# Attention and a squared-ReLU MLP on one core: earlier weight scans, row-tiled transposes in the second half, GpSimd sums tied to the softmax, float16 down products in four blocks

## Chip, cores and metric

The kernel runs on one core of one Trainium2 chip. The metric is the device time of one execution in microseconds (us). The kernel before takes 697.07 us (median of 3 runs, 697.04 to 697.47).

## What is computed

Attention over 4 batches, 8 heads, 576 positions and head size 64, with a bias from a small network on the positions, and then an MLP over the 2304 tokens. All inputs and outputs are float32.

```python
scores = scale * np.matmul(q, k.transpose(0, 1, 3, 2))
...
h = np.maximum(x @ w1 + b1, 0.0)
bias = h @ w2
scores = scores + bias.transpose(2, 0, 1)[None, :, :, :]
scores = scores - np.max(scores, axis=-1, keepdims=True)
attn = np.exp(scores)
attn = attn / (np.sum(attn, axis=-1, keepdims=True) + 1e-09)
return np.matmul(attn, v).astype(np.float32)
...
h = x @ w_in          # x: 2304 x 512, w_in: 512 x 2048
r = np.maximum(h, 0.0)
g = r * r
return (g @ w_out).astype(np.float32)   # w_out: 2048 x 512
```

## The kernel before, in words

**Units.** Attention is cut into units of one batch, one pair of heads and 128 query rows; a fifth unit of each pair holds the last 64 rows and is half as large. A *step* of the program handles one unit. The first half (steps 0 to 39) does batches 0 and 1 and also builds the bias; the second half (the loop from L1112, steps 40 to 82) does batches 2 and 3.

**First half.** A step multiplies q and k on TensorE (L425, into the PSUM tile `sp`, four banks). VectorE adds the bias and takes the row's extreme in one custom instruction per head (`reduce`, L438, tile `t` and column `negm`), ScalarE takes exp (L445, `p`). `transposes_by_rows` (L536) then transposes `p` in blocks of 64 rows and 128 columns (`half_block`, L534): two such blocks, in the upper and lower 64 rows of TensorE's array, go to two different PSUM banks. One last full block per unit, `pa` (L547), holds the columns of the tail. ScalarE copies the result to `pt` (L869), and `values` (L565) multiplies `pt` with v. Beside this run the pieces of the bias: masks (VectorE, L373), their products (TensorE, L383), and sums (ScalarE L388, VectorE L391, GpSimd L399). The order on TensorE is written by hand; at L856 `step` says what is issued in a step.

**Second half.** A step begins with the unit's scores. An even step then transposes the two units before it (`transposes`, L501): full blocks of 128 x 128 (L529), four to a bank. They use three banks (tags a, b, c), with `pa` of both units in the fourth (d), and the fourth group of blocks takes bank a again. ScalarE copies bank by bank (L1141). An odd step multiplies the transposed pair with v. The softmax of the step is issued after this. The tile `t` between VectorE and ScalarE has two buffers (`TB`). What is left of the engines is filled by a planner (`job` and `fill`, L946 to L964): each job is a list of pieces with an engine and a cost, and a step has so much `room` for VectorE and ScalarE. The jobs prepare the MLP. `scan` (L1009) takes the largest element of each w_in tile (VectorE, L204; 12 tiles here, 4 in steps 35 to 39 by `scan_first`), which sets a scale; `in_job` (L1084) splits w_in tiles into float16 high and low parts, with sums on GpSimd (`sums_in`, L738 to L740); `x_scaled` (L1035) does the same for the attention's result (`sums_x`, L797, on GpSimd; `high_x` L803, `low_x` L810).

**MLP.** 40 items, each a group of tokens and a block P (0 to 7) of the hidden columns. An item's up products (`products`, L1210, into `ha` and `hb`) are float16 products of high and low parts, in seven combinations (`sums`, L1214, adds them up again). `squares` and `parts_g` (L1240) make g = relu(h)^2 and split it into `gh` (ScalarE, L1246) and `gl` (VectorE, L1247), rounded float32 (`fp32r`). `down` (L1287, products L1302) adds gh·wh, gh·wl and gl·wh into `y`; 864 products of 128 x 512 in all. `leave` (L1260) takes `y` out. Tables (`lead_at`, `split_at`, `largest_at`, `raw_outs`, L1179 to L1187) say in which item a weight block is loaded and split. `high_out` and `rest_out` split w_out.

Of the kernel before, what the change touches and what calls it, by code (L numbers as in the profile page):

```python
# [27 lines left out]
AB = 2  # L28
# [43 lines left out]
MAGIC = 8388608.0  # L72

# [4 lines left out]
def attention_then_relu2_mlp(ctx: ExitStack, tc: tile.TileContext, q, k, v, cols, w_in, w_out, psi, xmat, dist, out):  # L78
# [11 lines left out]
    bank_p["p"] = aux_stack.enter_context(tc.tile_pool(name="aux", bufs=4, space=PSUM))  # L90

# [68 lines left out]
    def load_v(b, hp):  # L160
        t = att.tile([128, 5, 2, D], F32, name="v", tag="v", bufs=AB * HP)
        SP.dma_start(out=t, in_=v[b, hp])
        v_t[b, hp] = t
# [17 lines left out]
    small = keep.tile([128, 72], F32, name="small")  # L181
    used = [0]

    def column(w=1):
        used[0] += w
        return small[:, used[0] - w:used[0]]
# [32 lines left out]
    def power_of(ps_col):  # L219
# [3 lines left out]
        DVE.tensor_scalar(out=ti, in0=ti, scalar1=0x7F800000, scalar2=None, op0=ALU.bitwise_and)  # L223
        DVE.tensor_scalar(out=si, in0=ti, scalar1=-1.0, scalar2=266 * 2.0 ** 23, op0=ALU.mult, op1=ALU.add)
        DVE.tensor_scalar(out=isig, in0=top, scalar1=2.0 ** -12, scalar2=None, op0=ALU.mult)
# [7 lines left out]
    def top_w():  # L233
        m = column()
        mi = m.bitcast(I32)
        largest(wcols, m)
        DVE.tensor_scalar(out=m, in0=m, scalar1=HI_MIN, scalar2=HI_MAX, op0=ALU.max, op1=ALU.min)
        t = column()
# [194 lines left out]
    def reduce(u, n, negm, sp):  # L433
# [3 lines left out]
        t = att.tile([128, S], F32, name="t", tag="t", bufs=TB)  # L437
# [63 lines left out]
    def transposes(us, tags=None):  # L501
        next_tag = iter(tags) if tags else None
        groups = []
        pa = None
        for m, u in enumerate(us):
            p_of = p_t.pop(u)
            pt = att.tile([128, 9, 128], F32, name="pt", tag="pt", bufs=2)
            pt_t[u] = pt
            for h in range(2 if units[u][2] < TAIL else 1):
                groups.append((p_of, pt, h))  # L510
            groups.append((p_of, pt, None, m))
        if len(us) > 1:
            heads = [g for g in groups if g[2] is not None]
            groups = heads[:3] + [g for g in groups if g[2] is None] + heads[3:]
        last = []
        for p, pt, h, *m in groups:
            if h is None:
                if pa is None:
                    pa = bank("pa", "d" if tags and len(us) > 1 else next(next_tag) if tags else None)
# [207 lines left out]
    def high_out(n):  # L727
        copy_out(n)
        rest_out(n)
# [695 lines left out]
```

## Time and profile before

| | |
|---|---|
| median of 3 runs | 697.07 us |
| the profiled execution | 697.57 us |
| its span | 695.8 us |
| TensorE matmul (PE) | 676.8 us busy, 97% of the span |
| TensorE weight load (PEld) | 561.5 us, 81% |
| VectorE (DVE) | 549.9 us, 79% |
| ScalarE (ACT) | 473.2 us, 68% |
| GpSimd (POOL) | 196.5 us, 28% |

The span lies 1.8 us below the profiled execution's time, which counts what lies around the span. Busy time is the time in which an engine had at least one instruction at work; it is an average over three stages that do different work, so each stage is read by itself below. PE and PEld run side by side. Line numbers (L529) are those of the kernel before, unless the changed kernel is named. In a row, `out<-in` gives the tiles by the program's names, `x` the number of instructions; a number in brackets at the end of a timeline row is the idle time of the engine before it and what ended it.

### The profile page before, as it was taken

The numbers are of one execution on the slowest core, as the hardware profiler recorded it, in microseconds if no ns is written. First come the engines' busy times: TensorE is split into PE (matmuls) and PEld (weight loads), VectorE is DVE, ScalarE is ACT, GpSimd is POOL, SyncE is SP. The second block draws the span as 40 slices with busy tenths as digits, with TensorE's granted clock in tenths as the row PEclk, the third lists the DMA queues.
The fourth block names the chain that finished last, engine by engine and source line by source line (L and its number), as shares of the span: only waits on it lengthen the run. The fifth ranks groups of instructions, "written<-read, shape, count | busy, mean of one in ns | idle before, by whom it ended". The sixth has DMA issues, their size and how long they took to land.

```text
span 695.8 us, 17950 instructions
## 1 busy us (share of the span) xinstructions
PE 676.8 (97%) x7238; PEld 561.5 (81%) x7238; DVE 549.9 (79%) x1165; ACT 473.2 (68%) x960; POOL 196.5 (28%) x313
## 2 busy tenths in 40 slices
PE   6899999999999999999999999999999999999997
PEld 5578888887877878778788888888888888888886
DVE  8999989877788898998888969777477775567664
ACT  5678888888777989997666756766466664447221
POOL 6465545442112343653223205112020112001000
PEclk9999999999999999999999999999999999999999
DMA  6740000017476134111901443050057222633101
GB/s 188 205 128 13 20 2 3 2 63 206 152 266 196 55 116 131 47 33 57 367 2 62 152 167 122 14 214 1 1 194 291 106 77 106 227 121 122 62 1 31
DMA packets 31682, 75.16 MB, mean 108 GB/s; under 512 B 5616, under 2 KB 13936, under 8 KB 30576
## 3 DMA queue, kind: packets, MB, share of 16 engines
q1 hardware_dynamic: 31440, 73.76, 31.1%
q8 instruction: 57, 0.93, 0.6%
q14 instruction: 25, 0.20, 0.1%
q10 hardware_dynamic: 160, 0.26, 0.1%
HBM read 55.66 MB, written 18.35 MB: 106 GB/s over the span
## 4 chain that ended last, share of the span: by engine, by line
PE 86%; DVE 8%; ACT 2%; issue 2%; POOL 1%; DMA 0%; ACTq 0%; POOLq 0%; DVEq 0%
PE y L1302 29%; PE ha L1210 13%; PE sp L425 11%; PE px L565 10%; PE hb L1210 10%; PE bb L383 5%; PE pp L529 3%; PE pp L534 3%; DVE t L438 2%; DVE mask L373 1%; PE pa L547 1%; ACT pt L1141 1%; DVE bt L391 1%; ACT p L445 1%; DVE xT L496 0%
## 5 line engine op out<-in xcount | busy, mean ns | idle before, releaser
L1210 PEld LDWEIGHTS <-area 128*128 128x128 f16 x1680 | 147.7, 98 | 25.3 <-issue 8.4
L1302 PE MATMUL y<-w,gh 128*128 128x512 f32 x576 | 149.0, 398 | 0.6 <-ACT gh L1246 0.6
L1302 PEld LDWEIGHTS y<-w,gh 128*128 128x128 f32 x576 | 105.1, 188 | 22.2 <-ACT gh L1246 1.3
L438 DVE CUSTOM_DVE_ANT_0 t<-sp,area 128x576 f32<-128x576 f32 x144 | 104.2, 753 | 21.2 <-PE sp L425 10.3
L445 ACT ACTIVATE p<-t,negm 128x576 f32<-128x576 f32 x144 | 112.9, 794 | 2.7 <-DVE negm L438 2.1
L425 PE MATMUL sp<-k,q 64*128 64x288 f32 (+1 forms) x640 | 99.4, 428 | 5.5 <-DVE negm L438 3.9
L565 PE MATMUL px<-pt,v 128*64 128x128 f32 (+1 forms) x1600 | 92.2, 266 | 0.0
L565 PEld LDWEIGHTS px<-pt,v 128*64 128x64 f32 x1600 | 79.2, 137 | 10.7 <-ACT pt L1141 6.0
L1210 PE MATMUL ha<-area 128*128 128x256 f16 (+1 forms) x816 | 85.1, 260 | 0.7 <-DVE c L1227 0.7
L399 POOL TENSOR_TENSOR area<-bt,bt 128x256 f32<-128x256 f32 x72 | 65.9, 922 | 64.1 <-DVE bt L391 63.9
L1302 PE MATMUL y<-w,gl 128*128 128x512 f32 x288 | 79.0, 390 | 0.0
L425 PEld LDWEIGHTS sp<-k,q 64*128 64x128 f32 (+1 forms) x640 | 53.3, 176 | 25.5 <-issue 6.0
L1210 PE MATMUL hb<-area 128*128 128x256 f16 (+1 forms) x612 | 64.7, 260 | 0.0
L1302 PEld LDWEIGHTS y<-w,gl 128*128 128x128 f32 x288 | 54.1, 188 | 12.2 <-DVE gl L1247 0.2
L373 DVE TENSOR_TENSOR mask<-sdist,theta 128x1024 f16<-128x1024 f16 x81 | 57.3, 711 | 1.0 <-PE bb L383 0.8
L869 ACT COPY pt<-pp 128x512 f32<-128x512 f32 (+1 forms) x76 | 37.4, 544 | 24.9 <-PE pp L534 24.7
L383 PEld LDWEIGHTS <-mask 128*128 128x128 f16 x1296 | 45.9, 99 | 9.5 <-DVE mask L373 6.4
L383 PE MATMUL bb<-wmov,mask 128*128 128x64 f16 x1296 | 47.5, 193 | 5.5 <-DVE mask L373 4.7
L1141 ACT COPY pt<-pp 128x512 f32<-128x512 f32 x76 | 41.4, 601 | 12.8 <-PE pp L529 12.3
L1247 DVE TENSOR_TENSOR gl<-area,gh 128x512 fp32r<-128x512 f32 (+1 forms) x40 | 25.3, 668 | 27.3 <-ACT gh L1246 25.5
L738 POOL TENSOR_TENSOR raw<-wa 128x256 f32<-128x256 f32 x16 | 12.2, 761 | 120.9 <-issue 66.1
L388 ACT ACTIVATE bt<-bb,small 128x256 f32<-128x256 f32 x81 | 39.1, 486 | 7.1 <-PE bb L383 5.2
(164 smaller groups left out, 1062.2 us busy)
## 6 DMA issues: line engine op xcount, KB each, us to landing
raw<-in_w_in SPq DMA_DIRECT2D x32, 512.0 KB, 4.4
r<-in_w_out SPq DMA_DIRECT2D x16, 512.0 KB, 5.4
xs<-area SPq DMA_DIRECT2D x4, 1792.0 KB, 11.1
py<-o SPq DMA_DIRECT2D x12, 512.0 KB, 4.1
o<-py SPq DMA_DIRECT2D x12, 512.0 KB, 4.1
v<-in_v SPq DMA_DIRECT2D x16, 320.0 KB, 4.0
q<-in_q SPq DMA_DIRECT2D x32, 128.0 KB, 3.0
out<-o SPq DMA_DIRECT2D x8, 512.0 KB, 2.9
```

Of the source, the lines that this page charges most:

```text
L373: DVE.tensor_tensor(out=out, in0=win, in1=th, op=ALU.is_ge)
L383: PE.matmul(bb[:, 64 * (7 - r):64 * (8 - r)], lhsT=m[:, r], rhs=wmov[:, n], start=(n == 0), stop=(n == 1))
L388: ACT.activation(out=sv, in_=bv[:, 1], func=AF.Identity, scale=bscale)
L399: POOL.tensor_tensor(out=dst, in0=tw, in1=sw, op=ALU.add)
L425: mm = PE.matmul(out_t[to, x, :HALF], lhsT=qt[rows, cols], rhs=kt[rows, k0:k0 + HALF], start=True, stop=True)
L438: DVE.tensor_tensor_reduce(out=t.rearrange("p (x n) -> p x n", x=2), in0=sp[:, :, :HALF], in1=bias.rearrange("p (x n) -> p x n", x=2), sca ...
L445: ACT.activation(out=p[:, S * n:S * n + S], in_=t, func=AF.Exp, bias=negm[:, n:n + 1], scale=-1.0, accum_out=sums[:, 2 * ic + n:2 * ic + n ...
L565: PE.matmul(px[64 * h:64 * h + 64, 128 * m:128 * m + w], lhsT=vt[:, c, h], rhs=src, start=(c == 0), stop=(c == 4))
L869: ACT.copy(dst, src)
L1141: ACT.copy(*c)
L1210: PE.matmul(h[:, s, :w], lhsT=a, rhs=x, start=(k == 0), stop=(k == 5))
L1302: PE.matmul(y_t[n][k], lhsT=(gl if m == 2 else gh)[:, slot, o:o + 128], rhs=wl if m == 1 else wh, start=((n, P) in firsts and f == 0 and m ...
```

## The change

Five parts.

1. **Scans.** The 12 scans of w_in that were jobs of the second half are issued in steps 8 to 23 of the first half (`scan_corners`); the tiles are loaded from step 5 into four corners of the buffer `area`. The four of `scan_first` stay at its place. The second half's weight jobs begin at its first step (`begin`).
2. **Transposes.** `pair_by_rows` takes the place of `transposes` in the second half: half blocks as in the first half, banks a and b for the first unit, c and d for the second; then `pa` of both, into bank a, once ScalarE's copy of that bank is done.
3. **Buffers of `t`.** Four instead of two in the second half.
4. **GpSimd's sums.** `sums_in` and `sums_x` are issued just ahead of a step's softmax (a new slot "TT" of the planner, 2.0 us of room), and 26 one-column VectorE memsets make GpSimd wait until VectorE is there. The planner also keeps a count of how far GpSimd is behind.
5. **Float16 down products.** In blocks P = 4 to 7 the parts of g and w_out are float16, scaled by powers of two: gh·hi, gh·lo and gl·fine, where `fine` is hi/1024. This concerns 432 of 864 products. The scales need the largest element of eight w_out tiles (eight more scans on VectorE, in items 3 to 9), some 40 one-column VectorE instructions, five small products, eight more GpSimd and eight more ScalarE instructions on w_out tiles (the scaling and `fine`); the output is scaled as it leaves `y`.

```diff
+    scan_stack, scan_steps = ExitStack(), (8, 9, 11, 12, 14, 15, 17, 18, 20, 21, 22, 23)
...
+    def scan_corners(s):
+        if s == 5:
+            for k in range(4):
+                fetch(ins[k], corner[k])
+        if s in scan_steps:
+            k = scan_steps.index(s)
+            scan_w(k)
+            if k + 4 < CORNERS:
+                fetch(ins[k + 4], corner[k % 4])
...
+    def pair_by_rows(us, tags):
...
+            pp = [bank("pp", tag) for tag in tags[2 * m:2 * m + 2]]
+            n = 8 if units[u][2] < TAIL else 4
+            for c in range(n):
+                for x in range(2):
+                    half_block(pp[x][:, 64 * c:64 * c + 64], p, x, c // 4 * (S + 64) + c % 4 * 128)
+            for x in range(2):
+                yield pts[m][:, :n, 64 * x:64 * x + 64], pp[x][:, :64 * n].rearrange("p (c m) -> p c m", c=n)
+        pa = bank("pa", tags[0])
+        for m, u in enumerate(us):
+            PE.transpose(pa[:, 128 * m:128 * m + 128], p_t.pop(u)[:, S - 64:S + 64], ident)
+        for m, pt in enumerate(pts):
+            yield pt[:, 8], pa[:, 128 * m:128 * m + 128]
...
-                for m, c in enumerate(transposes(us, iter("bacb" if s == NA else "abca")) if us else ()):
+                for c in pair_by_rows(us, "bacd" if s == NA else "abcd") if us else ():
                     ACT.copy(*c)
...
+            t = soft_p["p"].tile([128, S], F32, name="t", tag="t", bufs=4)
...
-            ("POOL", 2.0, lambda: sums_in(n)),
+            ("TT", 1.45, lambda: sums_in(n, (0, 1), True)),
+            ("TT", 0.45, lambda: sums_in(n, (2,), True)),
...
+            fill(s, 4)
             for fn in sms:
                 fn()
...
+        t = home[n].tile([128, 3, 512], F16, name=f"w{n}", tag=f"w{n}", bufs=1)
+        hi, lo, fine = w_t[n] = [t[:, k] for k in range(3)]
+        POOL.tensor_scalar(out=a, in0=a, scalar1=oscale[0], scalar2=None, op0=ALU.mult)
+        ACT.copy(hi, a)
+        POOL.tensor_tensor(out=lo, in0=a, in1=hi, op=ALU.subtract)
+        ACT.activation(out=fine, in_=hi, func=AF.Identity, scale=1.0 / FINE)
...
+            if P >= NP // 2:
+                gl, gh = (mlp.tile([128, 4, 256], F16, name=x, tag=x, bufs=2)[:, 0:2, :w] for x in ("gl", "gh"))
+                g = c[:, 1 - f:4:2]
+                ACT.activation(out=gh, in_=g, func=AF.Identity, scale=1.0 / FINE)
+                DVE.scalar_tensor_tensor(out=gl, in0=gh, scalar=-FINE, in1=g, op0=ALU.mult, op1=ALU.add)
...
-                y_t[n][k], lhsT=(gl if m == 2 else gh)[:, slot, o:o + 128], rhs=wl if m == 1 else wh,
+                y_t[n][k], lhsT=(gl if m == 2 else gh)[:, slot, o:o + 128], rhs=(wh, wl, *fine)[m] if fine else (wh, wl, wh)[m],
```

**TensorE's order in an even step of the second half.** `sp` is the score tile, `pp` and `pa` the transposed blocks, `rp` a small product of the row sums. Before:

```order
L425 MATMUL sp<-k_4811,q_4814 128x288 x4
L474 LDWEIGHTS parts
L474 MATMUL rp<-ident_b,parts 128x128
L529 MATMUL pp<-ident,p 128x128 x12
L521 MATMUL pa<-ident,p 128x128 x2
L529 MATMUL pp<-ident,p 128x128 x4
L425 MATMUL sp<-k_4811,q_4814 128x288 x4
```

Now, with the line numbers of the changed kernel:

```order
L433 MATMUL sp<-k_4907,q_4910 128x288 x4
L485 LDWEIGHTS parts
L485 MATMUL rp<-ident_b,parts 128x128
L514 MATMUL pp<-ident,p 128x64 x32
L547 MATMUL pa<-ident,p 128x128 x2
L433 MATMUL sp<-k_4907,q_4910 128x288 x4
L566 MATMUL px<-pt,v 64x128 x20
```

Sixteen full blocks have become 32 half blocks, and the two `pa` blocks stand last, straight ahead of the next scores.

**VectorE's order in a step of the first half.** L438 (now L449) is the softmax pass; `mask` and `bt` belong to the bias; `xT` is the attention's result. Before:

```order
L438 ISA t,negm<-sp,area 128x576
L438 ISA negm 128x1
L438 ISA t,negm<-sp,area 128x576
L438 ISA negm 128x1
L373 TENSOR_TENSOR mask<-sdist,theta 128x1024
L391 TENSOR_TENSOR bt_2480<-bb,xc 128x256
```

Now:

```order
L449 ISA t,negm<-sp,area 128x576
L449 ISA negm 128x1
L449 ISA t,negm<-sp,area 128x576
L449 ISA negm 128x1
L209 TENSOR_REDUCE small<-area 128x1
L381 TENSOR_TENSOR mask<-sdist,theta 128x1024
L399 TENSOR_TENSOR bt_2501<-bb,xc 128x256
```

The scan (L209) has come in between the softmax and the bias work of the step.

**VectorE's order in a step of the second half**, in the changed kernel, at one of the memsets. `wa` is a w_in tile in preparation, `raw` the tile that GpSimd's sums go to:

```order
L205 SCALAR_TENSOR_TENSOR wa<-r_4403,wa 128x512
L206 SCALAR_TENSOR_TENSOR wa<-r_4403,wa 128x512
L750 MEMSET raw 128x1 x2
L449 ISA t,negm<-sp,area 128x576
L449 ISA negm 128x1
```

The memsets stand ahead of the softmax, and GpSimd's sums, which before began once their inputs were there, now begin after these.

## Rows read from the trace of the kernel before

**Rows 1.** Windows by stage: length, busy us (instructions) per engine, clock, DMA share, GB/s.

```profile
core 0: us, PE busy (x) PEld busy (x) DVE busy (x) ACT busy (x) POOL busy (x), PEclk, DMA share, GB/s
55.40:119.74 64.34, 64.33 (x1230) 55.51 (x1228) 58.16 (x142) 55.05 (x145) 31.94 (x34) 1.00 0.03 7
181.85:324.30 142.45, 139.24 (x1635) 112.40 (x1632) 125.48 (x319) 124.68 (x308) 51.17 (x110) 1.00 0.36 116
350.00:640.00 290.00, 290.00 (x1906) 243.07 (x1905) 211.36 (x340) 173.98 (x236) 48.66 (x56) 1.00 0.32 116
```

**Rows 2.** Timeline of PE, second half: start us, us, instruction.

```profile
258.63 1.24 PE L425 MATMUL sp<-k,q 64*128 64x288 f32 x8
259.87 1.48 PE L529 MATMUL pp<-ident,p 128*128 128x128 f32 x12
261.19 0.38 PE L521 MATMUL pa<-ident,p 128*128 128x128 f32 x2
261.41 0.60 PE L529 MATMUL pp<-ident,p 128*128 128x128 f32 x4
261.94 1.24 PE L425 MATMUL sp<-k,q 64*128 64x288 f32 x8
265.69 1.19 PE L425 MATMUL sp<-k,q 64*64 64x288 f32 x8
268.93 1.24 PE L425 MATMUL sp<-k,q 64*128 64x288 f32 x8
272.43 1.24 PE L425 MATMUL sp<-k,q 64*128 64x288 f32 x8
275.42 0.96 PE L425 MATMUL sp<-k,q 64*128 64x288 f32 x5
```

**Rows 3.** Timeline of VectorE and ScalarE, the same even step.

```profile
260.71 0.75 DVE L438 CUSTOM_DVE_ANT_0 t<-sp,area 128x576 f32<-128x576 f32 x1
260.57 0.59 ACT L1141 COPY pt<-pp 128x512 f32<-128x512 f32 x1 [0.23 <-PE pp L529]
```

**Rows 4.** Timeline of PE, first half.

```profile
111.90 0.66 PE L534 MATMUL pp<-ident,p 64*128 64x64 f32 x16
112.49 0.33 PE L547 MATMUL pa<-ident,p 128*128 128x128 f32 x1
```

**Rows 5.** Waits, second half: us in total, times, longest us.

```profile
ACT pt L1141 <- PE pp L529: 12.3, 15, 2.5
DVE t L438 <- ACT p L445: 7.2, 8, 1.6
```

**Rows 6.** Lines of PE and PEld, whole span: busy us, mean ns of one | idle before.

```profile
L529 PEld LDWEIGHTS pp<-ident,p 128*128 128x128 f32 x304 | 33.3, 140 | 4.5 <-issue 1.8 <-ACT p L445 1.6 <-ACT wa L195 0.4
L534 PEld LDWEIGHTS pp<-ident,p 64*128 64x128 f32 x544 | 22.5, 140 | 7.4 <-issue 1.3 <-ACT xT L576 0.9 <-ACT bt L388 0.4
L1302 PE MATMUL y<-w,gh 128*128 128x512 f32 x576 | 149.0, 398 | 0.6 <-ACT gh L1246 0.6
L1302 PE MATMUL y<-w,gl 128*128 128x512 f32 x288 | 79.0, 390 | 0.0
```

**Rows 7.** Timeline of PE, MLP.

```profile
520.13 1.98 PE L1302 MATMUL y<-w,gh 128*128 128x512 f32 x8
521.95 1.07 PE L1302 MATMUL y<-w,gl 128*128 128x512 f32 x4
522.86 2.79 PE L1210 MATMUL ha<-xT,area 128*128 128x256 f16 x24
525.49 2.13 PE L1210 MATMUL hb<-xT,area 128*128 128x256 f16 x18
527.37 1.40 PE L1302 MATMUL y<-w,gh 128*128 128x512 f32 x5
```

**Rows 8.** Lines of VectorE, second half.

```profile
L204 DVE TENSOR_REDUCE small<-raw 128x1 f32<-128x512 f32 x12 | 7.6, 680 | 0.0
L223 DVE TENSOR_SCALAR small<-small 128x1 int32<-128x1 int32 x3 | 0.5, 153 | 0.1
```

**Rows 9.** Timeline of VectorE, first half.

```profile
103.20 0.76 DVE L438 CUSTOM_DVE_ANT_0 t<-sp,area 128x576 f32<-128x576 f32 x1 [0.33 <-PE sp L425]
112.11 0.76 DVE L438 CUSTOM_DVE_ANT_0 t<-sp,area 128x576 f32<-128x576 f32 x1 [0.34 <-PE sp L425]
```

More of the change, by code (lines that the diff above doesn't have):

```diff
@@ L185, in column @@
         used[0] += w
-        return small[:, used[0] - w:used[0]]
+        return columns[0][:, used[0] - w:used[0]]
+    columns = [small]
     def lead_w(n, a, upto=7):
@@ L499, in scale_x @@
         times_rows(b, hp, *spread_rows(rows_t))
[L501 to L519, printed above, removed]
-                at = slice(128 * m[0], 128 * m[0] + 128)
-                PE.transpose(pa[:, at], p[:, S - 64:S + 64], ident)
-                last.append((pt[:, 8], pa[:, at]))
-                if len(last) == len(us):
-                    yield from last
-            else:
-                pp = bank("pp", next(next_tag) if tags else None)
-                for c in range(4):
-                    k0 = h * (S + 64) + 128 * c
-                    PE.transpose(pp[:, 128 * c:128 * c + 128], p[:, k0:k0 + 128], ident)
-                yield pt[:, 4 * h:4 * h + 4], pp.rearrange("p (c m) -> p c m", c=4)
     def half_block(dst, p, x, k0):
@@ L962, in fill @@
                     j[0] = s + lag(eng, j[1][0][0])
+                if eng == "POOL":
+                    behind[0] = max(behind[0], 3.2 * s) + cost
+                    if j[1] and j[1][0][0] != "POOL":
+                        j[0] = max(j[0], int(behind[0] / 3.2) + 1)
         for js in (jobs, norms):
@@ L1037, in x_scaled @@
         if n == 0:
[L1038 to L1039 removed]
+            free = [xT[b][:, HP - 1, 0:512] for b in range(AB, B)]
             for k, ms in enumerate(((3, 1, 7), (4, 6), (2, 5))):
@@ L1112, in attention_then_relu2_mlp @@
     with tc.manual_schedule():
-        job(NA + 1, *(("DVE", 0.68, lambda k=k: scan(k)) for k in range(SCANS, NF)))
+        job(NA, ("DVE", 0.75, begin))
         x_job(NA + 4, 0)
@@ L1195, in attention_then_relu2_mlp, with scan_out, squares_of @@
     c_t, g_t, y_t = {}, {}, {}
-    scales = []
+    columns[0], used[0] = xT[0][:, 0, 384:512], 0
+    ocols, beta, lead_root = column(len(late_outs)), column(NB), column(NB)
+    root, root_beta = column(NB), column(NB)
+    oscale, reach = [], []
+    xcols.extend(column(HP) for _ in range(AB, NB))
+    def scan_out(n):
+        k = late_outs.index(n)
+        largest(wraw_t[n][:, :, :, 1].bitcast(F32), ocols[:, k:k + 1])
+    def squares_of(dst, cols):
+        DVE.tensor_tensor(out=dst, in0=cols, in1=cols, op=ALU.mult)
@@ new lines, in scale_columns, with early_columns @@
+    def scale_columns(n):
+        if n < B - 1:
+            return overall(xcols[n])
+        cols = column(1 + HP)
+        squares_of(cols[:, 1:], xcols[n])
+        largest(xcols[n], cols[:, 0:1])
+        return cols
+    def early_columns():
+        cols = column(NF + (B - 1) * HP)
+        values_of(wcols, cols[:, 0:NF])
+        squares_of(cols[:, 0:NF], wcols)
+        for n in range(B - 1):
+            squares_of(cols[:, NF + HP * n:NF + HP * n + HP], xcols[n])
+        return cols
@@ new lines, in told_x, with then, told_out @@
+    def told_x(n):
+        def then(ps):
+            scale_of(n, ps[:, 0:1])
+            if n >= B - 1:
+                roots_of(n, n + 1, ps[:, 1:])
+            if n == B:
+                last_scales(B, NB)
+        return then
+    def told_out(ps):
+        oscale.extend(power_of(ps, 0x7F000000, 11))
+        r = column()
+        DVE.tensor_scalar(out=r.bitcast(I32), in0=oscale[0].bitcast(I32), scalar1=0.5, scalar2=58.5 * 2.0 ** 23, op0=ALU.mult, op1=ALU.add)
+        oscale.append(r)
+        last_scales(0, B)
```

189 lines of the change are left out of this document (122 added, 67 removed).

## Prediction

> **What bounds the kernel now.** I read the windows by stage first, because a saving is worth only what its own stage lets through [rows 1]. In the first half, from 55.40 to 119.74 us, PE is busy for 64.33 of 64.34 us, but VectorE for 58.16 as well: TensorE is the bound with 6.2 us of VectorE to spare. In the second half, from 181.85 to 324.30 us, PE is busy 139.24 of 142.45 us, VectorE 125.48 and ScalarE 124.68: again TensorE, by a thinner margin (3.2 us of it are idle). In the MLP, from 350 to 640 us, PE is busy 290.00 of 290.00 us and VectorE only 211.36. So time is to be had from TensorE in all three stages, and work that is put on VectorE is free in the MLP, nearly free in the first half and costly in the second. The clock is granted in full (1.00) in all three, so no term below is a matter of clock. Next I read the timelines, for the cost of one instruction where TensorE runs without a gap, start to start; the busy times in the groups of instructions overlap and are no price.
>
> **The change part by part.**
>
> *Down products in float16.* Before: from 520.13 to 522.86 us twelve products of 512 columns, 0.2275 us each [rows 7]. What a float16 product costs is read from the up products behind them: (525.49−522.86)/24 = 0.1096 us, and (527.37−522.86)/42 = 0.1074 us, for 256 columns. Twice that is 0.2148 to 0.2192 us, so 8.3 to 12.7 ns less for each. For 432 of the 864 products (576 and 288 in [rows 6]) this is 3.6 to 5.5 us, all of it on the bound engine. I take **−4.5**. The work that comes with it lies on VectorE (eight scans at 0.68 us [rows 8] = 5.4 us, and some 40 one-column instructions at 0.153 us = 6.1 us) and on GpSimd and ScalarE (eight each). It is hidden by the 290 − 211 = 79 us in which VectorE idles in the MLP, so it costs nothing. Were that cover gone, it would be up to 11.5 us.
>
> *Row-tiled transposes.* Before: twelve full blocks in 261.19−259.87 = 1.32 us, 0.110 us each [rows 2]. The first half shows the other form: eight pairs of half blocks in 112.49−111.90 = 0.59 us, 0.074 us for what a full block does [rows 4]. The 304 full blocks [rows 6] thus give at most 304 × 0.036 = 10.9 us; with all of TensorE's idle time in this stage, 3.2 us, on top it is 14.1, the upper end.
> How much arrives depends on what ends an even step next. An even step now lasts 261.94−258.63 = 3.31 us [rows 2]. Its scores start at 258.63; the second softmax pass on them ends at 260.71+0.75 = 261.46 [rows 3]. The next scores overwrite the banks which that pass reads, so the loop from scores to softmax to scores can't be shorter than 2.83 us and a start-up. The step with less to transpose (272.43 to 275.42) lasts 2.99 us, and I take that as the floor: a gain of 0.32 us where TensorE alone would give 16 × 0.036 = 0.58. Of the 20 even steps, 13 have full units on all sides: 4.2 us. The seven others (one of them 268.93−265.69 = 3.24 us, whose own softmax is half as long) I put at 0.2 us each: 1.3 us. The wait of VectorE for a buffer of `t` (7.2 us in 8 waits [rows 5]) goes with four buffers, but most of it only moves to the next wait for ScalarE; I take a fifth, 1.5 us.
> What is late next is ScalarE. Before, `pa` had a bank of its own; now it stands behind the copy of bank a, and behind it on TensorE stand the next scores. The first copy of a pair now starts at 260.57 and takes 0.59 us [rows 3], so bank a is free at 261.16. The row-tiled blocks start at 259.87 and 16 pairs end at 259.87 + 16 × 0.074 = 261.05. That is 0.1 us of waiting if ScalarE is on time, with 0.38 us of `pa` behind it: 261.54, still near the 261.62 that the floor allows. ScalarE is not always on time: I take off 1.0 us (0.05 us in each even step). Together 4.2 + 1.3 + 1.5 − 1.0: **−6.0**, between −2 (only half of the first term) and −14.1.
>
> *Scans into the first half.* Twelve scans at 0.68 us [rows 8] are 8.2 us of VectorE. In the second half this leaves an engine that isn't the bound there and gives nothing by itself. In the first half it meets 6.2 us of slack in the stretch of steps 9 to 23 [rows 1]. Part of the slack is waiting for the scores of the very step, 0.33 and 0.34 us before the first softmax pass [rows 9], and a scan behind the second pass can eat into that only if the mask behind it isn't needed at once. The scans are spread over 16 steps, so each step gets 0.5 us against 6.2/15 = 0.4 us of slack. I take **+1.5**, between 0 and 8.2 (no cover at all). The loads of the scans (512 KB each) are moved ahead on SP's queue; the DMA share there is 0.03 [rows 1], so they land in time and delay nothing.
>
> *Memsets ahead of the softmax.* 26 one-column instructions; the nearest row is the one-column one at 0.153 us [rows 8], so 0 to 4.0 us of VectorE. They stand where VectorE mostly waits for the scores. **0**. GpSimd is busy 51 of 142 us [rows 1] and has room to start later.
>
> The sum is 1.5 − 6.0 − 4.5 = −9.0 us, against the profiled execution 697.57 − 9.0 = 688.6. That execution lies 0.5 us over the median of the runs, 697.07, so against the median it is **688.1 us**.
>
> **The rivals.**
>
> *VectorE becomes the bound of the first half.* For: 58.16 + 8.2 is 66.4 us in a stretch of 64.34 [rows 1]. Against: single waits show VectorE catching up. Then the scans cost 8.2 instead of 1.5: 697.07 + 8.2 − 6.0 − 4.5 = 694.8 us. Chance 0.13; in a third of it the second half also gives little, and the time is no different from before.
>
> *The transposes give all they have.* If the next scores don't wait for the softmax, and TensorE's idle time closes too: 697.07 + 1.5 − 14.1 − 4.5 = 680.0 us. For: VectorE loses 8.2 us of work in this stage. Against: the 2.99 us of the lighter step. Chance 0.10.
>
> *Float16 gains nothing.* If TensorE takes a product of 512 columns at the same 0.2275 us in either type: 692.6 us. For: the difference per product is a few ns, and the up products differ in shape from the down ones. Chance 0.07.
>
> *The memsets are not covered.* 4.0 us come back: 692.1 us. Chance 0.03.
>
> *ScalarE is late, and TensorE stands (slower).* `pa` waits for ScalarE's first copy, and the scores of the next step are queued behind it, so each us by which the copy is late is lost on TensorE and then on VectorE. With a mean lateness of L in 20 even steps the cost is 20 × L: it passes the 9.0 us of gain at L = 0.45 us. At 0.6 us the time is 697.07 − 9.0 + 12.0 = 700.1 us. For: ScalarE is busy 125 of 142 us [rows 1]. Against: before, ScalarE waited for TensorE ahead of the copies in 15 of the pairs, 12.3 us in all [rows 5], so it has been early, 0.8 us on the mean. Chance 0.05.
>
> *Weight loads set the pace (slower).* The rows: 304 full blocks kept the weight load busy 33.3 us, 0.110 us each, and the 544 half blocks 22.5 us, 0.041 us each [rows 6]. If a half block needed a whole load of 0.110 us after all, 608 of them would take 66.9 us, 33.6 more: 697.07 + 1.5 + 33.6 − 4.5 = 727.7 us. Against: the 0.041 us, and the 0.59 us of the eight pairs [rows 4], into which 16 such loads (1.76 us) don't fit. Chance 0.02. The Trainium skill has the rule behind this rival (TensorE: Matmul & The Clock Gate, on LDWEIGHTS): "A 32×128 weight load takes the same time as a 128×128 weight load". By that rule alone halving the rows saves no load and doubles their number; the trace doesn't agree, at 0.041 against 0.110 us, so I keep the rows.
>
> **How the numbers follow.** My forecast has a chance of 0.60; with the rivals' 0.13, 0.10, 0.07, 0.03, 0.05 and 0.02 that is 1. The bounds of its own terms reach from 697.07 − 10.9 − 5.5 = 680.7 to 697.07 + 1.5 − 2 − 3.6 = 693.0. The range, **681.5 to 695.0 us**, takes in nearly all of these, the float16 and the memset cases, and VectorE as the bound up to its 694.8; left out are the full gain (0.10), the two slower cases (0.07) and the worst third of the VectorE case (0.04). What a measurement of this kernel can tell from no change is about 0.2%, 1.4 us. Faster by more than that: all but the two slower cases and that third, 0.89. Within it: 0.04. Slower: 0.07.
>
> **What would show it.** In the first half the windows should show PE still near 100% of the stretch of steps 9 to 23 and that stretch no more than 1.5 us longer; if PE shows idle time that VectorE's masks or softmax ended, the scan term was too small. In the second half an even step should last about 3.0 us from scores to scores, with PE waiting for VectorE's `negm` and not for ScalarE's copy; a wait of `pa` on ScalarE is the slower rival. Twelve down products of blocks 4 to 7 should span 2.58 to 2.63 us instead of 2.73. The forecast is wrong if the stages move by other amounts than +1.5, −6.0 and −4.5, whatever the total does.

## The result and the profile after

The changed kernel takes 688.59 us (median of 4 runs, 688.39 to 689.58) against 697.27 for the kernel before in the same comparison: a ratio of 0.9875, 95% interval 0.9858 to 0.9892. The prediction was 688.1, range 681.5 to 695.0. The profiled execution took 688.39 us with a span of 686.6, so 9.2 us less than the span of before.

The total came out as forecast; its parts did not. The table cuts the spans of the profiled executions of all kernels at the same four points: the first score product of step 10, that of step 40, the first down product, and the end. Lines 1 and 2 are the two kernels, the rest are the experiments. The medians are of all runs of a kernel, the lengths are of its one profiled execution.

| kernel | median us | ratio to before, 95% interval | steps 10 to 39 | second half | MLP |
|---|---|---|---|---|---|
| before | 697.27 | | 123.11 | 152.85 | 361.05 |
| changed | 688.59 | 0.9875 (0.9858 to 0.9892) | 123.59 | 148.43 | 355.96 |
| full transposes | 690.74 | 0.9914 (0.9898 to 0.9931) | 123.59 | 150.39 | 355.63 |
| no early scans | 688.24 | 0.9876 (0.9861 to 0.9891) | 123.05 | 147.88 | 355.95 |
| dummy scans | 691.26 | 0.9917 (0.9901 to 0.9932) | 123.55 | 151.04 | 355.94 |
| two buffers of t | 690.14 | 0.9900 (0.9885 to 0.9915) | 123.52 | 149.79 | 355.79 |
| three parts undone | 691.74 | 0.9924 (0.9909 to 0.9938) | 123.55 | 151.92 | 355.64 |
| row tiling alone | 692.36 | 0.9931 (0.9915 to 0.9948) | 123.57 | 151.98 | 355.77 |
| fp32r down products | 694.60 | 0.9964 (0.9951 to 0.9977) | 123.52 | 148.44 | 361.69 |
| pa in the next step | 695.40 | 0.9980 (0.9970 to 0.9990) | 123.56 | 154.11 | 356.88 |
| pa in the last bank | 722.36 (one run) | | 123.56 | 181.76 | 356.51 |
| pa in score banks | 718.41 | 1.0312 (1.0293 to 1.0330) | 123.54 | 179.02 | 355.52 |
| pa copied by VectorE | 695.47 | 0.9981 (0.9972 to 0.9990) | 123.57 | 151.91 | 359.49 |
| scans in idle steps | 689.58 | 0.9892 (0.9875 to 0.9908) | 124.47 | 147.90 | 355.94 |

Where an edit does not touch a stage, its length repeats within 0.1 us in steps 10 to 39, within 0.6 us in the second half (147.88 to 148.44 in the kernels without early scans, with scans in idle steps and with fp32r down products, against 148.43) and within 0.9 us (mostly 0.4) of the changed kernel's MLP; the one exception is the MLP of experiment 9. So the stages tell parts apart that the totals blur, but a difference of half a microsecond in the second half tells nothing by itself. The stretch before step 10 is not in the table: it ended between 58.31 and 59.86 us, with nothing changed there in most of these kernels.

From before to after: steps 10 to 39 +0.48, second half −4.42, MLP −5.09, and −0.13 ahead of step 10 (−0.62 up to the end of step 3, which is no work of the change, see "The start" below; +0.47 in steps 8 and 9). The windows of the changed kernel, by stage as in [rows 1]; the last row is the whole second half:

```profile
55.09:120.11 65.02, 64.36 (x1231) 55.42 (x1228) 63.58 (x153) 55.44 (x145) 31.91 (x34) 1.00 0.22 72
350.00:640.00 290.00, 290.00 (x1944) 216.24 (x1943) 220.79 (x399) 180.56 (x247) 60.25 (x63) 1.00 0.32 116
182.21:330.64 148.43, 140.57 (x2047) 109.64 (x2044) 125.99 (x346) 129.89 (x324) 57.30 (x117) 1.00 0.28 91
```

The same whole second half before:

```profile
181.85:334.70 152.85, 148.35 (x1743) 119.97 (x1739) 134.26 (x333) 130.66 (x316) 58.10 (x117) 1.00 0.38 124
```

TensorE has 7.8 us less work in the second half (148.35 to 140.57), and the stage is only 4.4 us shorter: its idle time rose from 4.5 to 7.9 us. VectorE has 8.3 us less.

An even step of the changed kernel, timeline of PE:

```profile
211.13 1.24 PE L433 MATMUL sp<-k,q 64*128 64x288 f32 x8
212.31 0.23 PE L485 MATMUL rp<-ident_b,parts 128*128 128x128 bf16 x1
212.47 1.22 PE L514 MATMUL pp<-ident,p 64*128 64x64 f32 x32
213.91 0.44 PE L547 MATMUL pa<-ident,p 128*128 128x128 f32 x2 [0.22 <-ACT pt L1168]
214.28 0.46 PE L433 MATMUL sp<-k,q 64*64 64x288 f32 x2
```

And ScalarE and VectorE in it:

```profile
213.27 2.05 ACT L1168 COPY pt<-pp 128x512 f32<-128x512 f32 x4 [0.43 <-PE pp L514]
213.21 0.75 DVE L449 CUSTOM_DVE_ANT_0 t<-sp,area 128x576 f32<-128x576 f32 x1
```

The step lasts 214.28 − 211.13 = 3.15 us; the same one took 3.30 before, and the floor of the prediction was 2.99. The 32 half blocks are done before 213.7. Then `pa` stands until ScalarE has copied the first bank. ScalarE isn't late there: it stands idle for 0.43 us ahead of that copy, until TensorE has filled the bank. The half blocks alternate between two banks, so the first bank is full only with the 16th half block, and its copy starts 2.14 us after the scores, where it started 1.94 us after them in a step of the kernel before [rows 2] [rows 3]. In 12 of the 20 even steps ScalarE waits so for TensorE, 0.3 us or more, and `pa` then waits for ScalarE. The waits of the second half, 182.21 to 320 us (engine, line, waited for: us, times, longest):

```profile
PEld pa L547 <- ACT pt L1168: 5.0, 13, 0.6
PE pa L547 <- ACT pt L1168: 3.0, 11, 0.5
DVE t L449 <- ACT p L456: 1.3, 1, 1.3
```

The wait for `t`, 7.2 us in 8 waits before [rows 5], is nearly gone; the wait of `pa` is new (3.35 us on TensorE with the three waits that are too short for this list).

In the MLP, timeline of PE, one item of block 4 to 7:

```profile
581.59 1.89 PE L1422 MATMUL y<-w,gh 128*128 128x512 f16 x8
583.32 1.03 PE L1422 MATMUL y<-w,gl 128*128 128x512 f16 x4
584.18 1.89 PE L1422 MATMUL y<-w,gh 128*128 128x512 f16 x8
585.91 1.03 PE L1422 MATMUL y<-w,gl 128*128 128x512 f16 x4
586.77 2.78 PE L1318 MATMUL ha<-xT,area 128*128 128x256 f16 x24
589.39 2.13 PE L1318 MATMUL hb<-xT,area 128*128 128x256 f16 x18
591.36 1.89 PE L1422 MATMUL y<-w,gh 128*128 128x512 f16 x8
```

Its 24 down products take 586.77 − 581.59 = 5.18 us, 216 ns each.

### The profile page after: what moved, and what is told of

It reads as the page before. It is cut to its first block, busy times and chain, and to the rows that moved or that the text cites. A ratio compares the mean times of both kernels' runs of the same rounds, so it can differ in the third digit from the quotient of the medians.

```text
span 686.6 us, 18664 instructions
## 1 busy us (share of the span) xinstructions
PE 663.6 (97%) x7546; PEld 515.9 (75%) x7546; DVE 555.5 (81%) x1243; ACT 477.4 (70%) x976; POOL 208.2 (30%) x321
## 4 chain that ended last, share of the span: by engine, by line
PE 80%; DVE 11%; ACT 6%; issue 2%; DMA 0%; POOL 0%; DVEq 0%; ACTq 0%; POOLq 0%
PE y L1422 28%; PE ha L1318 13%; PE sp L433 10%; PE hb L1318 10%; PE px L566 9%; PE bb L391 4%; PE pp L514 4%; DVE t L449 2%; ACT pt L1168 2%; DVE mask L381 2%; ACT p L456 2%; PE pa L527 1%; DVE bt L399 1%; DVE area L824 1%; PE pa L547 0%
## 5 line engine op out<-in xcount | busy, mean ns | idle before, releaser
L1422 PE MATMUL y<-w,gh 128*128 128x512 f32 (+1 forms) x576 | 143.6, 389 | 0.6 <-ACT gh L1365 0.3
L449 DVE CUSTOM_DVE_ANT_0 t<-sp,area 128x576 f32<-128x576 f32 x144 | 103.7, 752 | 17.7 <-PE sp L433 10.9
L1422 PE MATMUL y<-w,gl 128*128 128x512 f32 (+1 forms) x288 | 77.3, 385 | 0.0
L1422 PEld LDWEIGHTS y<-w,gh 128*128 128x128 f32 x288 | 52.5, 188 | 11.5 <-ACT gh L1365 0.8
L751 POOL TENSOR_TENSOR raw<-wa 128x256 f32<-128x256 f32 (+1 forms) x48 | 31.0, 675 | 99.2 <-issue 55.1
L514 PEld LDWEIGHTS pp<-ident,p 64*128 64x128 f32 x1144 | 45.6, 139 | 12.8 <-issue 1.9
L895 ACT COPY pt<-pp 128x512 f32<-128x512 f32 (+1 forms) x76 | 37.4, 544 | 25.6 <-PE pp L514 25.4
L514 PE MATMUL pp<-ident,p 64*128 64x64 f32 x1144 | 49.9, 226 | 1.6 <-ACT rows L490 0.7
L1422 PEld LDWEIGHTS <-gh 128*128 128x128 f16 x288 | 27.9, 98 | 30.2 <-ACT gh L1358 0.8
L1168 ACT COPY pt<-pp 128x512 f32<-128x512 f32 (+1 forms) x83 | 39.6, 557 | 11.4 <-PE pp L514 11.2
```

Source lines behind the costliest of these rows:

```text
L449: DVE.tensor_tensor_reduce(out=t.rearrange("p (x n) -> p x n", x=2), in0=sp[:, :, :HALF], in1=bias.rearrange("p (x n) -> p x n", x=2), sca ...
L514: PE.transpose(dst, p[rows, k0:k0 + 128], ident[rows, rows])
L895: ACT.copy(dst, src)
L1168: ACT.copy(*c)
L1422: PE.matmul(y_t[n][k], lhsT=(gl if m == 2 else gh)[:, slot, o:o + 128], rhs=(wh, wl, *fine)[m] if fine else (wh, wl, wh)[m], start=((n, P) ...
```

## Experiments

Each starts from the changed kernel. "Stretch" is the second half of the table, 148.43 us there.

**1. Full transposes.** The function `transposes` of before is called again, with its banks.

```diff
-                for c in pair_by_rows(us, "bacd" if s == NA else "abcd") if us else ():
+                for c in transposes(us, iter("bacb" if s == NA else "abca")) if us else ():
```

> Only the transposes of the second half go back to full blocks (304 of 128 x 128, pa in a bank of its own, norm rows in banks c and b); scans, buffers, memsets and float16 products stay as in the changed kernel. Theory A (TensorE's work is what the second half gained): the 4.4 us that the second half gained come back nearly whole, about 692.5 us. Rival B (VectorE, rid of 12 scans and with four buffers of t, carried the gain): at most 1 us comes back, under 689.5 us.

The stretch grew to 150.39, so 1.96 us of the 4.42 came back: neither theory. The transposes alone explain less than half of the gain, and something else carries the rest.

**2. Dummy scans.** Twelve more VectorE passes, one for every third step from step 41.

```diff
+        for m in range(CORNERS):
+            job(NA + 1 + 3 * m, ("DVE", 0, lambda: largest(area[:, 27 * S:27 * S + 512], small[:, 76:77])))
```

> Twelve extra scans on VectorE in the second half (512 columns each, as those that were there before; one in every third step from the second on, their result unused). Theory A (the scans' leaving is what gave the part of the second half's gain that full transposes kept, 2.3 us): 690 to 691 us. Rival B (VectorE has the room; that part is of the four buffers or of the sums' place): 688.4 us within 0.5.

The stretch grew to 151.04, by 2.61 us. Theory A, a little more: twelve scans of 0.67 us, 8.0 us by their own lengths, raise VectorE's busy time by 4.9 us (125.99 to 130.89) and cost 2.6 us on the path, although VectorE is not the busiest engine. Step by step, cut at the first score products, the scans in steps 55 and 60 lengthen those steps by 0.60 and 0.75 us, as much as a scan is long; those in steps 44, 47, 50, 56, 68, 71 and 74 lengthen nothing (0.01 us or less). These are not the steps of the 12 scans of before, which all stood in steps 41 to 47.

**3. Two buffers of t.** `bufs=4` becomes `bufs=2` in the second half.

> The softmax tile t has two buffers again in the second half; nothing else. Forecast of the prediction: 1.5 us comes back, 689.9 us. Theory A (the four buffers carry the 2.3 us): 690.5 us or more. Rival B (the wait only moves to ScalarE): 688.4 us within 0.5.

The stretch grew to 149.79, by 1.36: the forecast's term (1.5) was the right size. The total, 1.5 us over the changed kernel's, agrees.

**4. Three parts undone, and 5. row tiling alone.** Both have two buffers and the dummy scans; the first has full transposes as well.

> Three parts undone at once: full transposes, two buffers of t, and twelve extra scans in the second half. What stays of the change there is the place of GpSimd's sums with its memsets and the planner's rules. In the runs with one part undone the second half, from the first scores of step 40 to the first down product, took 150.39, 149.79 and 151.04 us, against 148.43 in the changed kernel and 152.85 before; the losses (1.96, 1.36, 2.61) add up to 5.93 where 4.42 were gained. Theory A (the parts overlap: each undone alone loses what the others can't use without it): 152.5 to 153.2 us. Rival B (they add up and the sums' new place costs 1.5 us): 154 to 154.7 us.

> Two parts undone: two buffers of t and twelve extra scans in the second half; the row-tiled transposes stay. The same stretch: theory A (row-tiled transposes need VectorE's relief to show, since the even step ends with the softmax or with ScalarE's copy): 152 to 153 us, next to nothing of the 8 us that TensorE is spared. Rival B (they are worth their 1.96 us by themselves): 150.5 to 151.2 us.

151.92 and 151.98 us. With both other parts undone, row tiling is worth nothing (−0.06); with both in place it is worth 1.96. That is theory A of both, each a little under its range. The windows over the whole second half, first with the three parts undone, then with row tiling alone:

```profile
182.41:334.33 151.92, 148.11 (x1744) 119.80 (x1740) 130.64 (x358) 130.18 (x316) 57.77 (x117) 1.00 0.26 87
```

```profile
183.35:335.33 151.98, 141.49 (x2048) 110.24 (x2044) 131.19 (x358) 131.00 (x324) 58.05 (x117) 1.00 0.27 88
```

TensorE is spared 6.6 us of work (148.11 to 141.49) and the stage does not move: all of it turns into idle time, 10.5 us in place of 3.8. What ends part of it, by the waits of the kernel with row tiling alone:

```profile
DVE t L449 <- ACT p L456: 7.6, 8, 2.5
PEld sp L433 <- DVE negm L449: 4.7, 10, 1.0
PE sp L433 <- DVE negm L449: 3.1, 10, 0.7
PE pa L547 <- ACT pt L1170: 2.9, 11, 0.5
```

VectorE waits for a buffer of `t`, TensorE waits for VectorE's `negm` (3.1 us, against 1.0 with the three parts undone) and for the copy ahead of `pa`. So the parts are one chain. By pairs of kernels that differ in one part: the scans are worth 2.61 us with four buffers and 2.19 with two (151.98 − 149.79); the buffers 1.36 without the extra scans and 0.94 with them; row tiling 1.96 or nothing. The two prices of the scans, and of the buffers, differ by less than the 0.6 us that this stage moves by itself; the two of row tiling do not. Scans and buffers together are worth 1.53 us without row tiling (151.92 − 150.39) and 3.55 with it (151.98 − 148.43). With the three undone the stretch is still 0.93 us shorter than before. All of that lies behind the loop: from the first scores of step 40 to those of step 79 it took 134.30 us before and 134.38 with the three undone, and from there to the first down product 18.55 against 17.54 (17.55 in the changed kernel). There the up products of the second item waited for VectorE before:

```profile
328.87 2.68 PE L1210 MATMUL ha<-area 128*128 128x256 f16 x23 [0.69 <-DVE c L1227]
```

In the changed kernel they follow without a wait:

```profile
325.09 2.67 PE L1318 MATMUL ha<-area 128*128 128x256 f16 x23
```

Which of the rest of the change frees VectorE there (the sums' place, the memsets, the planner's rules, scans spread more evenly) was not taken apart.

**6. pa in the bank that is copied last**, a doubled wait: `tags[3]` in place of `tags[0]`.

> pa goes into the bank that ScalarE copies last instead of the one it copies first, so it waits three copies longer (2.06 us for four copies, 0.515 each, in the changed kernel: 1.5 us). Theory A (what pa waits is lost on TensorE, 20 even steps, less what the softmax loop covers): 1.0 to 1.5 us in each even step, 708 to 718 us. Rival B (the loop of scores and softmax covers it): under 695 us.

The stretch grew by 33.33 us to 181.76, 1.67 us for each of 20 even steps, more than theory A said:

```profile
PE pa L547 <- ACT pt L1168: 29.3, 19, 1.7
```

On TensorE 26.3 us of waiting ahead of `pa` (29.3 in place of 3.0) go with 33.3 us on the stretch, so such a long wait is lost in full, and the odd steps grow as well, by 0.56 us on the mean (3.47 to 4.03). The rival of the prediction on the slower side is a real mechanism with a price near the one stated (20 × L); in the changed kernel L is 3.35/20 = 0.17 us.

**7. pa in the next step.** The two blocks stand in the odd step, behind its scores; the products that need them come last.

```diff
+                for c in pair_tails(us, "a") if us and us[0] in p_t else ():
+                    ACT.copy(*c)
                 pieces = values(us, "d") if us else []
```

> The two pa blocks of a pair are issued in the next, odd step, behind its scores and ahead of its value products, in bank a, which ScalarE has long copied by then; the value products that use them come last in the step. Nothing else changes. Theory A (the 3.35 us that TensorE waits ahead of pa are lost on the path, at the price of 1.67 us per even step and 1.5 us of lateness that the run with the last bank showed): 685 to 687 us, with no wait of pa for ScalarE. Rival B (the loop of scores, softmax and scores ends the even step anyway, and pa lengthens the odd step, which TensorE bounds): 688.5 to 690 us.

Slower: the stretch is 154.11. The timeline of PE shows both halves of it:

```profile
213.03 1.24 PE L433 MATMUL sp<-k,q 64*128 64x288 f32 x8
214.21 0.23 PE L485 MATMUL rp<-ident_b,parts 128*128 128x128 bf16 x1
214.37 1.22 PE L514 MATMUL pp<-ident,p 64*128 64x64 f32 x32
216.02 1.19 PE L433 MATMUL sp<-k,q 64*64 64x288 f32 x8 [0.43 <-DVE negm L449]
217.14 0.44 PE L549 MATMUL pa<-ident,p 128*128 128x128 f32 x2
```

The even step is at 216.02 − 213.03 = 2.99 us, the floor that the prediction took, now waiting 0.43 us for `negm`. But the odd step, which TensorE bounds here, grew from 3.70 to 4.07. Over the whole loop the even steps lose 0.32 us on the mean (3.17 to 2.85) and the odd ones gain 0.60 (3.47 to 4.07): more than the two blocks themselves take (0.37), since steps 45, 55 and 75 grow by 1.1 to 1.8 us; the value products now wait for the copies of `pa` as well, 2.2 us in 5 waits. That is rival B, and worse than it said.

**8. pa in spare columns of the score banks.** Of the 512 columns of each score bank 224 are unused; `pa` goes there, ahead of the half blocks, and its copies stand first and third on ScalarE.

```diff
+            pa = sp4[:, 2 * m, 384:512]
+            PE.transpose(pa, p_t.pop(us[m])[:, S - 64:S + 64], ident)
```

> The two pa blocks of a pair no longer wait for ScalarE's first copy: each goes to columns 384 to 511 of a score bank of the same step, the first ahead of its unit's half blocks, the second between the two units; ScalarE copies them first and third. Theory A (the 3.35 us that TensorE waits for ScalarE ahead of pa are lost on the path): 685 to 686 us, and no wait of pa for ScalarE in the trace. Rival B (the softmax loop ends the step anyway): 688.4 us within 0.5, the wait returns at the scores as a wait for negm. Rival C (the scores now wait for the copies of pa): slower, over 689 us.

179.02 us in the stretch, rival C by far. The wait that did it is on another engine than the one named there:

```profile
DVE t L451 <- ACT pt L1178: 31.3, 18, 2.5
```

VectorE's softmax now waits for ScalarE's copies of `pa`, though they read other columns: the bank is shared, and the program guards it as one. Over the whole second half there are 20 such waits, and each ends 0.03 us after a copy of `pa`. The Trainium skill (PSUM — Partial Sum Buffer, "PSUM bank collisions raise a hardware error") has the reason: the compiler's scheduler puts a dependency between any two instructions of different engines that touch the same bank and the same quarter of the partitions, reads and writes alike. This run agrees, at 31.3 us, for two reads.

**9. pa copied by VectorE**, behind the softmax of the step; and the first four scan loads written in steps 5, 6, 8 and 9.

> Two trials in stages of their own. First half: the first four loads for the scans are issued in steps 5, 6, 8 and 9 instead of all in step 5; theory A (TensorE's stall in step 8, 0.23 us in the changed kernel and 1.0 us in the run without scans, comes from the full DMA): step 8 lasts 3.0 us again; rival: 3.3. Second half: the copies of pa move from ScalarE to VectorE, behind the softmax of the step; theory A (ScalarE is what is late): the stretch of 148.43 us falls to 146.5 to 148; rival B (VectorE's time is dearer, as the dummy scans showed: 8.2 us of it cost 2.6): 149 to 152 us.

151.91 us in the stretch: rival B, but not by VectorE's working time alone. In its place behind the softmax VectorE also stands and waits for `pa`:

```profile
DVE pt L1179 <- PE pa L547: 6.3, 12, 0.9
```

The MLP also grew, by 3.5 us. In 2.4 us of it TensorE waits for work that VectorE is behind with (1.6 us for `area`, 0.8 us for `xT`); the rest is not explained. In the first half step 8 lasted 3.02 us, as theory A said, but not for its reason: the four loads were issued together at 43.80 us all the same (see experiment 11).

**10. No early scans.**

```diff
-            scan_w(k)
+            if k == 0:
+                DVE.memset(wcols[:, 0:CORNERS], 0.2)
```

> The 12 scans in the first half are left out and their 12 maxima are set to a constant (the loads stay, so does all else). Theory A: the first half ends 0.9 to 1.0 us earlier (the sum of the four steps 8, 9, 13 and 23 that grew by 0.29, 0.18, 0.26 and 0.22), about 687.5 us, and the early gain of 0.6 us in step 3 is no matter of the scans. Rival B (the scans cost nothing, the steps grew from the moved loads or from chance): no change, 688.4 us.

Steps 10 to 39 fell from 123.59 to 123.05, so the scans cost 0.54 us there, and 0.18 in step 9 (3.52 to 3.34, as before). The total hardly moved (688.24), because step 8 lasted 4.39 us in this execution, against 3.31 in the changed kernel and 3.02 before: with the 0.29 us of step 8 the theory had counted as scan what is not scan. So theory A's cost is there at a little over half its size, and the total of rival B comes from step 8 and not from free scans. The longer step 8 comes near the stretch in which the moved loads fill the DMA. Before, 46 to 52 us:

```profile
46.00:52.00 6.00, 6.00 (x140) 4.87 (x139) 5.55 (x13) 4.29 (x14) 4.54 (x6) 1.00 0.10 20
```

In the changed kernel:

```profile
46.00:52.00 6.00, 6.00 (x141) 4.99 (x139) 5.31 (x12) 4.89 (x15) 3.98 (x6) 1.00 0.97 368
```

In the run without scans more than the scans is different: no scan holds the later loads back, so SyncE issues all twelve from 43.21 to 60.13 us, and the DMA is still full in the stretch behind (52 to 57 us, where its share is 0.37 in the changed kernel):

```profile
43.21 8.63 SPq L695 DMA_DIRECT2D area<-in_w_in  x7
53.97 6.16 SPq L695 DMA_DIRECT2D area<-in_w_in  x5
```

```profile
52.00:57.00 5.00, 4.00 (x59) 3.16 (x61) 3.62 (x10) 3.22 (x11) 1.96 (x3) 1.00 1.02 392
```

There TensorE stood for 1.0 us in step 8 with nothing that the profile shows to wait for:

```profile
53.36 0.99 PE L433 MATMUL sp<-k,q 64*128 64x288 f32 x6 [1.00 <-issue]
```

In the other kernels with these loads step 8 lasted from 3.01 us up to this 4.39. That the full DMA delays TensorE's own instructions would be one reading, but the DMA's share in the first microsecond of step 8 doesn't follow the lengths: 0.76 with step 8 at 3.02 us (experiment 9), 0.96 at 3.31 (changed kernel), 0.42 at 3.84 (dummy scans), 0.99 at 4.39. The cause stays open.

**11. Scans in idle steps.**

```diff
-    scan_stack, scan_steps = ExitStack(), (8, 9, 11, 12, 14, 15, 17, 18, 20, 21, 22, 23)
+    scan_stack, scan_steps = ExitStack(), (8, 11, 12, 14, 15, 17, 17, 18, 20, 20, 21, 22)
```

> The changed kernel with the scans placed elsewhere in the first half: none in steps 9, 13 and 23, which grew by 0.18, 0.26 and 0.22 us, and two each in steps 17 and 20, where VectorE still idles 0.89 and 0.30 us in the changed kernel; the first four loads in steps 5, 6, 8 and 9. Theory A (the scans cost what VectorE's idle time of their own step does not cover): from step 10 to step 40 at most 0.15 us over the 123.11 us of before (123.59 in the changed kernel), 687.5 to 688.2 us in all. Rival B (VectorE is full across steps, and wherever the scans stand they cost 0.5 us or more): 123.5 us or more. Step 8 with the loads apart: 3.0 us, as in the last run.

A miss: 124.47 us from step 10 to step 40, 0.9 us more than in the changed kernel, and steps 9, 13 and 23 are as long as with a scan of their own. The 0.9 us stand in steps 19 and 21 (0.35 and 0.55 us longer), behind the two steps with two scans. So VectorE's idle time of one step was the catching up from others; it carries a backlog from step to step, and two scans close together only make it longer. The loads were not apart either, and step 8 lasted 3.50 us where 3.0 was expected. SyncE waits for nothing between them, so it issues all four at once, wherever they stand:

```profile
43.35 1.85 SPq L695 DMA_DIRECT2D area<-in_w_in  x4
```

**12. fp32r down products** in all eight blocks; the scans of w_out and the scales stay and are unused.

```diff
-            if P >= NP // 2:
+            if False:
```

> All 864 down products in rounded float32 again, with the w_out parts and g parts of the kernel before; the eight scans of w_out and the columns of scales are still made, and unused. Theory A (a float16 product costs 216 ns in place of 232, and an item's up products 0.07 us more behind it): 5.1 us come back, 693.5 us. Rival B (the MLP gained from another part, the later loads or the order of the items): under 690 us.

The MLP grew from 355.96 to 361.69, by 5.73 us; theory A, a little more. It is 0.64 us longer than before. That is the most that the machinery of the scales can be said to cost: an MLP that no edit touches moves by up to 0.9 us as well, so the cost itself is not shown. The timeline of PE, one item:

```profile
580.12 2.79 PE L1318 MATMUL ha<-xT,area 128*128 128x256 f16 x24
582.75 2.13 PE L1318 MATMUL hb<-xT,area 128*128 128x256 f16 x18
584.64 2.09 PE L1422 MATMUL y<-w,gh 128*128 128x512 f32 x8
586.57 1.08 PE L1422 MATMUL y<-w,gl 128*128 128x512 f32 x4
587.49 1.98 PE L1422 MATMUL y<-w,gh 128*128 128x512 f32 x8
589.30 1.07 PE L1422 MATMUL y<-w,gl 128*128 128x512 f32 x4
590.21 2.03 PE L1318 MATMUL ha<-xT,area 128*128 128x256 f16 x17
```

24 products take 590.21 − 584.64 = 5.57 us, 232 ns each, against 216 in float16; the 42 up products take 4.52 us here and 591.36 − 586.77 = 4.59 behind float16.

## Why the prediction was right, and where it was not

**The total** was right to 0.5 us, and that is partly luck: −4.4 where −6.0 stood, +0.35 where +1.5 stood (+0.97 without the 0.62 us that the start gave and not the change), −5.1 where −4.5 stood. Each lies inside its own bounds, but the prediction called itself wrong "if the stages move by other amounts", and by that sign its account of both halves of the attention was.

**Float16 down products: right mechanism, low by a fifth.** The term was 10.4 ns for each product; an item shows 16. The price of the float16 product was right (215 to 219 ns expected, 216 measured; twelve take 2.59 us, as the sign said). The price of the rounded float32 one was too low: it came from twelve products in a row that ran at 227.5 ns [rows 7], and the twelve of an item that stand ahead of them take longer, 5.57 us for all 24, 232 ns each. The item gives back 0.07 us on the up products behind. Whether "it costs nothing" was wrong is open: at most 0.64 us, which is inside what an untouched MLP moves by.

**The scans' new place: the cost was right in kind, their leaving was not.** They cost 0.48 us in steps 10 to 39 (0.54 by the run without them) and 0.18 in step 9, 0.7 in all, inside the stated 0 to 8.2 and nearer its lower end than the 1.5 that I took. The 0.68 us of a scan is its own length and too high a price: with eleven of them in steps 9 to 23, VectorE's busy time there rose by 5.4 us (58.16 to 63.58), 0.49 each. The step that failed is "In the second half this leaves an engine that isn't the bound there and gives nothing by itself". Twelve scans put back there cost 2.2 to 2.6 us, the largest price of the three parts. That is the price in the steps of experiment 2; that the old place in steps 41 to 47 cost as much is not shown by itself, but with the three parts undone the loop is as long as before to 0.1 us. In a loop where TensorE waits for VectorE's `negm` and VectorE for ScalarE's buffer, each engine is busy for 85 to 97% of the stage and no one of them is the bound: it changes from step to step, and a scan in a step where VectorE is late is lost whole (steps 55 and 60 of experiment 2), one in another step not at all.

**Row-tiled transposes: the loop behind the floor was right, the sum was not.** Where `pa` no longer stood ahead of the scores, the even step did end with the wait for `negm`, at 2.99 us (experiment 7). But 2.99 is not the shortest: other full even steps of that kernel last 2.83 to 2.94 us, and the lighter steps 46 and 66 of the changed kernel 2.79, with a wait for `negm` at their end. Step 66, from its scores to the next:

```profile
270.59 1.24 PE L433 MATMUL sp<-k,q 64*128 64x288 f32 x8
273.38 0.51 PE L433 MATMUL sp<-k,q 64*128 64x288 f32 x2 [0.28 <-DVE negm L449]
```

The step shown under the result stands at 3.15. The step of the prediction that failed there is the time of the first copy, which was taken over from the order of before ("bank a is free at 261.16", 2.53 us after the scores; 2.72 measured). The wait for it was put at 0.05 us in each even step as ScalarE's lateness and is 0.22 in the one shown, 0.17 on the mean, while ScalarE itself waits for TensorE's half blocks. The sign set for the slower rival, a wait of `pa` on ScalarE, is thus there, at a small price. Of the "−6.0", 4.5 belonged to the transposes less that lateness and 1.5 to `t` (seven steps at 0.2 us are 1.4, not 1.3); measured, row tiling is worth 1.96 at best, and nothing where VectorE isn't relieved as well, a condition that the prediction did not have. The price per block held: in the step shown the first 15 of the 16 pairs take 0.066 us each, start to start, where 0.074 was taken [rows 4]. The rival of the full gain, 14.1 us, fell with it.

**Buffers of t**: 1.5 taken, 1.36 measured, and 0.94 with the extra scans.

**Memsets and the place of GpSimd's sums**: nothing taken. No run takes them out, so that 0 is not tested. The rival of 4.0 us was out of reach, since a memset lasts 59 ns where 153 were taken, 1.5 us for all 26:

```profile
L750 DVE MEMSET raw<- 128x1 f32 x16 | 0.5, 59 | 0.1
```

**The rivals.** VectorE as the bound of the first half came near: it is busy 63.58 of 65.02 us, and the scans took nearly all its slack, at 0.7 us. Float16 without gain fell. Weight loads as the pace fell: the 1144 half-block loads keep the weight load busy for 45.6 us, 0.040 each:

```profile
L514 PEld LDWEIGHTS pp<-ident,p 64*128 64x128 f32 x1144 | 45.6, 139 | 12.8 <-issue 1.9 <-ACT rows L490 1.1 <-ACT p L456 0.9
```

The second number of the row corrects what the prediction said of the rule that it quoted from the Trainium skill: one load of 64 rows lasts 139 ns, one of 128 rows lasted 140 [rows 6]. So the trace agrees with that rule: a single load is no shorter. What falls is only the doubling of the time, because the loads of the two row groups run side by side: in the even step shown the two of a pair start 3 to 7 ns apart. That halves the busy time for each; why it falls still further, from 0.110 to 0.040, was not taken apart.

**The start.** Step 3 ended at 36.66 us, 0.6 us earlier than before. That is no work of the change: in the kernels whose edit comes later it ended anywhere from 36.63 to 38.65 us. In the step ahead of it, after an idle stretch of 2.24 us, the scores ran at a granted clock of 0.57 before (near the lower of the two levels) and of 0.90 in the changed kernel's profiled execution. Before:

```profile
28.44 2.10 PE L425 MATMUL sp<-k,q 64*64 64x288 f32 x8 [2.24 <-DVE negm L438]
```

After:

```profile
28.51 1.33 PE L433 MATMUL sp<-k,q 64*64 64x288 f32 x8 [2.24 <-DVE negm L449]
```

That the slower scores are what made step 3 later is argued from this, not shown by a run of its own. With step 8 this start spreads the end of the first ten steps over 1.6 us, and no cause is read here from totals that differ by less.

## What to carry to other kernels

Where three engines hand one another work in a ring, with each of them busy for more than four fifths of the time, a part's price depends on the others: here less work for TensorE alone moved nothing, relief for VectorE alone (no extra scans, four buffers) gave 1.5 us, and both together 3.5. Cost such parts together, and test them by undoing each alone and all at once; the two differ just where the parts overlap. When an engine seems late, look what it waited for itself: here the copy was late because the order of the blocks filled its bank late. Ahead of moving work from one step to the next, ask what ends each of them: where another loop ends the step, taking work out gains little, and where the engine itself ends it, work put in is paid in full.

## What the runs showed of the hardware

A float16 product of 512 columns took 216 ns and one in rounded float32 227 to 232 ns, start to start. Weight loads of different row groups overlapped (pairs 3 to 7 ns apart), though one lasted as long as a full one (139 against 140 ns). Two engines that read different columns of one PSUM bank wait for each other in the program as built (31.3 us in 18 waits). The queue issued the four loads in one row, at 43.35 and 43.80 us, though they were written in four steps: nothing in it waited for the steps between them.
